# Issuing the output stores of a fused cross-covariance attention and mixture-of-adapters kernel from one queue, with the last outputs in seven pieces

## The chip, the cores and the metric

The kernel runs on one core of a Trainium2 chip. The metric is the device time of one execution in microseconds (us), lower is better. The kernel before takes 256.47 us, the median of three runs (256.42 to 256.54).

## What is computed

The inputs q, k and v are [4, 6400, 256] in float32. For each of the four batches, the columns of q and k are normalised over the 6400 tokens, a 256 x 256 matrix of their products goes through a softmax over its rows, and v is multiplied by it. The 25600 rows that come out then go through a mixture of eight adapters of rank 16, of which each row uses its best two:

```python
qn = q / (norm(q, axis=1) + 1e-6);  kn = k / (norm(k, axis=1) + 1e-6)
a  = softmax(kn.transpose(0, 2, 1) @ qn / tau)        # [4, 256, 256]
x  = (v @ a).reshape(25600, 256)
w  = softmax of the two largest of x @ w_gate          # 8 experts
out = x + sum over those two e of w_e * ((x @ A[e]) @ B[e])
```

The output is 25600 x 256 in float32, 26.2 MB.

## The kernel before

**Tiles.** A batch's 6400 tokens are 50 chunks of 128 (token = 50 x partition + chunk). Two chunks make a pair; there are 100 pairs, numbered u = 0 to 99, 25 to a batch. Pairs go in groups of five, for which gating is worked out at once; the last batch's are of 5, 5, 5, 5, 3 and 2 pairs. In this text G0 to G17 are the eighteen groups of pairs 0 to 89, five pairs each.

**Stages.** First the products and squares of batch 0 (`gram`, `norm`, `square`) run as its q and k arrive. Then a loop over slots takes one pair a slot: TensorE transposes its part of v (`transposes`, copied out of PSUM by VectorE or ScalarE), works out z (`z_gz`, L470), transposes the gated z back (`gz_t`, L494; copied by VectorE at L500, or from slot 100 on by ScalarE at L498), and adds both products into y (`y_mm` L486, `delta` L506). Beside that, up to slot 67, the loop carries the products of the following batch. The order of all instructions is written out by hand, and each engine runs its own in that order.

**Loads.** GpSimd issues all loads of q, k and v but the first; they convert float32 to bfloat16 on their way.

**Stores.** ScalarE copies each pair's y from PSUM into its group's tile `ys` (L510), 2 KB of each partition for a pair. A full group of five is 128 rows of 10,240 bytes, 1,280 KB. `delta` appends the full group to the list `unsent`, and `send`, called once a slot after `delta`, issues the oldest while more than `keep` are unsent. `keep` is 7 up to slot 67 and falls by one every four slots to 0 at slot 95. While `keep` is not 0 ScalarE issues the store, and SyncE when it is 0. By this ScalarE issues G0 to G14 and SyncE G15, G16 and G17. ScalarE issues in the order of its own program, between its copies; SyncE has nothing else to do, so its issues go out as soon as what they wait for is there. The last ten pairs, 90 to 99, are stored one at a time by SyncE at L513, 256 KB each, straight after their copies. They are called s0 to s9 here.

**Semaphores.** The 33 DMAs that SyncE and ScalarE issue (five first loads of SyncE, eighteen groups, ten single pairs) share eight completion semaphores in turn. A DMA that takes a semaphore waits until the DMA that had it before, eight places earlier, has landed: until all sixteen increments of that one have come, one from each of the sixteen DMA engines. s5 has the semaphore of G14 before it.

**Buffers.** `ys` has nine buffers. A group's first copy waits until the store of the group nine tiles earlier has landed.

Of the kernel before, what the change touches and what calls it, by code (L numbers as in the profile page):

```python
# [16 lines left out]
def kernel(  # L17
# [16 lines left out]
    nc = tc.nc  # L34
# [11 lines left out]
    NPAIR = NC // 2  # L46
    NPT = B * NPAIR
    GRP = 5
# [11 lines left out]
    out_v = out.rearrange("(b p c) d -> b p c d", b=B, p=P)  # L60
# [23 lines left out]
    for b, (first, last) in GRAM.items():  # L84
        n = last - first + 1
# [30 lines left out]
    def piece(kind, c):  # L116

        if kind == "qk":
            return divmod(c, PC)
        s = 0  # L120
        while c >= VP[s]:
            c -= VP[s]
            s += 1
        return s, c

    def used(kind, b, c, n):
        left[kind][where[kind, b, piece(kind, c)[0]]] -= n
# [220 lines left out]
    free_banks = [False]  # L348
    unsent = []

    def transposes(g, eng):

        b, p = divmod(g, NPAIR)
        gr = groups[g]
        if "vT" not in gr:
            gr["vT"] = vt_pool.tile([P, CC, 2 * GRP, P], BF16, tag="vT", name="vT")
        s, o = piece("v", 2 * p)
        vt = tiles["v"][b, s]
        full = ps_t.tile([P, 512], FP32, tag="pt", name="vT_ps")
        pt = full[:, 0:256].bitcast(BF16).rearrange("p (c t) -> p c t", c=CC)  # L360
        i = 0
        for sc in range(2):
            for ic in range(CC):
                nc.tensor.matmul(pt[:, ic, sc * P:(sc + 1) * P],  # L364
                                 vt[:, o + sc, ic * P:(ic + 1) * P], ident,
                                 is_transpose=True, start=(i == 0), stop=(i == 3))
                i += 1
        used("v", b, 2 * p, 2)
        w = 2 * (g - gr["f"])
        dst = gr["vT"][:, :, w:w + 2, :]  # L370
        src = pt.rearrange("p c (s t) -> p c s t", s=2)
        if eng == "act":
            nc.scalar.copy(dst, src)  # L373
        else:
            nc.vector.tensor_copy(dst, src)  # L375
        gr["full"] = full
        pr[g] = {"vT": dst, "w": w}
# [125 lines left out]
    def delta(u):  # L503
        r, gr = pr.pop(u), groups[u]
        for sc in range(2):
            nc.tensor.matmul(r["y"][:, sc, :], r["gzT"][:, sc, :], ball_sb, start=False,  # L506
                             stop=(sc == 1), skip_group_check=True)
        if "ys" not in gr:
            gr["ys"] = y_pool.tile([P, 2 * GRP, C], FP32, tag="ys", name="ys")
        nc.scalar.copy(gr["ys"][:, r["w"]:r["w"] + 2, :], r["y"])  # L510
        if u >= NPT - 2 * GRP:
            c0 = 2 * (u % NPAIR)
            nc.sync.dma_start(out_v[gr["b"], :, c0:c0 + 2, :], gr["ys"][:, r["w"]:r["w"] + 2, :])  # L513
        elif u == gr["f"] + gr["n"] - 1:
            unsent.append(gr)

    def send(keep):


        eng = nc.scalar if keep else nc.sync  # L520
        while len(unsent) > keep:
            gr = unsent.pop(0)
            c0, n = 2 * (gr["f"] - gr["b"] * NPAIR), 2 * gr["n"]
            eng.dma_start(out_v[gr["b"], :, c0:c0 + n, :], gr["ys"][:, 0:n, :])
# [43 lines left out]
    while nz < NPT or zq is not None or dq is not None:  # L568
# [12 lines left out]
        u = None  # L581
        if nz < min(slot, NPT) and groups[nz]["ready"]:
            u = nz
# [7 lines left out]
        if slot < NPT and not behind:  # L591
            transposes(slot, "dve" if items or f is chain3 else "act")
        if dq is not None:
            delta(dq)
        dq, zq = zq, u
        send(max(0, min(DEFER, DEFER - (slot - GRAM[B - 1][1]) // 4)))
        if behind:
            deal(0.3)
# [52 lines left out]
```

## Time and profile before

| | |
|---|---|
| median of three runs | 256.47 us (256.42 to 256.54) |
| the profiled execution's own time | 256.67 us |
| its span in the profile | 254.9 us |
| mean granted TensorE clock | 0.971 |
| busy: TensorE matmul, ScalarE, VectorE, GpSimd | 219.1, 176.3, 152.6, 32.5 us |
| bytes read from and written to HBM | 78.91 and 26.21 MB |
| store queue of ScalarE (q10): packets, MB | 2160, 19.66 |
| queue of SyncE (q1): packets, MB | 3488, 7.87 |
| ScalarE's last copy of y (L510) ends | 246.3 us |

The profile is of one execution. Times are from the start of its span. Sixteen DMA engines move all transfers; each queue has a ring on every one of them, and a store of 128 rows puts eight rows on each. A row is one packet; after its rows each engine writes one packet of 4 bytes, the increment of the semaphore. The share of DMA in a table is the mean busy share of the sixteen; it can pass 1 a little, since the packets of one engine overlap by 4 ns. "SPq" and "ACTq" stand for the issuing sequencers of SyncE and ScalarE, and "landing" is the time from issue to the last increment.

### The profile page before, as it was taken

Reading aid. Unit: us, or ns where it says so; the run is one execution under the profiler, and the core shown is the slowest. Engines: PE = TensorE matmul, PEld = TensorE weight load, DVE = VectorE, ACT = ScalarE, POOL = GpSimd, SP = SyncE. Lnnn points to the kernel's source line nnn. Section 1 sums busy time; section 2 is a strip of 40 time slices with the busy share of each in tenths; the row PEclk is TensorE's granted clock in tenths of the full one; section 3 lists DMA queues with packets and bytes.
Section 4 is the critical chain, followed back from the end, with each engine's and each line's share of the span. In section 5 each row is a group of like instructions: output and inputs, shape, how many; then the busy total and the mean of one; then the engine's idle time right before and its main releaser. Section 6 shows DMA issues by size and latency. Waiting matters only on the chain.

```text
span 254.9 us, 7402 instructions
## 1 busy us (share of the span) xinstructions
PE 219.1 (86%) x3106; PEld 189.2 (74%) x3106; DVE 152.6 (60%) x577; ACT 176.3 (69%) x290; POOL 32.5 (13%) x67
## 2 busy tenths in 40 slices
PE   0787792986999999999999999989999899999950
PEld 0444460875998878989999779879997799999930
DVE  1322335463757769676686685747587876778720
ACT  2434344676687797877976978778866777887850
POOL 8031221121112102020111011000000200000000
PEclk9999998697999999999999999999999999999996
DMA  7999999999999999999999999999999999999986
GB/s 210 225 215 216 212 217 214 213 215 216 213 213 215 221 209 214 221 209 218 211 219 213 214 297 233 259 270 284 252 299 295 382 331 356 425 425 418 425 359 231
DMA packets 14177, 66.80 MB, mean 262 GB/s; under 512 B 2624, under 2 KB 2752, under 8 KB 10816
## 3 DMA queue, kind: packets, MB, share of 16 engines
q0 software_dynamic: 8496, 38.80, 74.6%
q10 hardware_dynamic: 2160, 19.66, 18.7%
q1 hardware_dynamic: 3488, 7.87, 8.5%
q8 instruction: 24, 0.39, 0.6%
q14 instruction: 9, 0.07, 0.1%
HBM read 78.91 MB, written 26.21 MB: 412 GB/s over the span
## 4 chain that ended last, share of the span: by engine, by line
DMA 43%; PE 43%; DVE 5%; ACT 2%; POOL 2%; issue 2%; DVEq 0%; ACTq 0%; POOLq 0%
DMA vt<-in_v_dram 21%; PE y_ps L486 11%; DMA qk<-in_k_dram 9%; DMA qk<-in_q_dram 8%; PE acc L217 7%; PE y_ps L506 5%; DMA out_dram<-ys 5%; PE zg L470 5%; PE vT_ps L364 5%; PE zg L494 3%; PE vT_ps L385 3%; PE nrm L234 2%; DVE gz L474 1%; PE nrm L228 1%; POOL qk L148 1%
## 5 line engine op out<-in xcount | busy, mean ns | idle before, releaser
L207 ACT ACTIVATE sq<-qk 128x1024 bf16<-128x1024 bf16 x87 | 89.6, 1054 | 22.7 <-DMA qk<-in_k_dram 17.4
L217 PE MATMUL acc<-qk 128*128 128x256 bf16 x400 | 74.1, 286 | 15.3 <-DMA qk<-in_k_dram 8.8
L510 ACT COPY ys<-y_ps 128x512 f32<-128x512 f32 x100 | 58.7, 587 | 22.8 <-PE y_ps L506 19.3
L486 PE MATMUL y_ps<-a_bf,vT 128*128 128x256 bf16 x400 | 59.9, 272 | 0.3 <-ACT ys L510 0.3
L217 PEld LDWEIGHTS <-qk 128*128 128x128 bf16 x400 | 34.3, 101 | 25.2 <-DMA qk<-in_k_dram 11.4
L474 DVE TENSOR_TENSOR gz<-zg,gate 128x256 bf16<-128x256 f32 x100 | 41.7, 418 | 14.4 <-PE zg L470 12.9
L375 DVE COPY vT<-vT_ps 128x512 bf16<-128x512 bf16 x63 | 26.7, 424 | 29.0 <-PE vT_ps L364 28.3
L364 PE MATMUL vT_ps<-ident,vt 128*128 128x128 bf16 x400 | 39.5, 222 | 2.2 <-DMA vt<-in_v_dram 1.9
L234 PEld LDWEIGHTS <-sq 128*128 128x128 bf16 x600 | 36.1, 98 | 7.0 <-ACT sq L207 3.0
L470 PE MATMUL zg<-wa_sb,vT 128*128 128x128 bf16 x400 | 38.5, 219 | 1.2 <-DVE gzT L500 1.0
L506 PE MATMUL y_ps<-ball_sb,gzT 128*128 128x256 bf16 x200 | 38.2, 273 | 0.0
L234 PE MATMUL nrm<-ones_bf,sq 128*128 128x1 bf16 x600 | 35.7, 165 | 1.2 <-ACT sq L207 1.2
L486 PEld LDWEIGHTS <-vT 128*128 128x128 bf16 x400 | 33.5, 97 | 3.1 <-issue 0.4
L364 PEld LDWEIGHTS <-vt 128*128 128x128 bf16 x400 | 30.0, 99 | 5.2 <-DMA vt<-in_v_dram 2.7
L373 ACT COPY vT<-vT_ps 128x512 bf16<-128x512 bf16 x37 | 21.7, 587 | 10.2 <-PE vT_ps L364 8.9
L494 PE MATMUL zg<-ident,gz 128*128 128x128 bf16 x200 | 27.7, 221 | 1.1 <-DVE gz L474 0.6
L470 PEld LDWEIGHTS <-vT 128*128 128x128 bf16 x400 | 26.0, 97 | 3.3 <-issue 2.2
L500 DVE COPY gzT<-zg 128x256 bf16<-128x256 bf16 x90 | 25.3, 281 | 0.0
L148 POOL DMA_DIRECT2D qk<-in_q_dram x21 | 11.5, 547 | 88.4 <-ACT sq L207 19.4
L209 DVE TENSOR_TENSOR sq<-qk 128x1024 bf16<-128x1024 bf16 x13 | 9.1, 697 | 22.2 <-DMA qk<-in_k_dram 14.2
L151 POOL DMA_DIRECT2D vt<-in_v_dram x17 | 9.0, 534 | 65.7 <-PE y_ps L506 49.2
L494 PEld LDWEIGHTS <-gz 128*128 128x128 bf16 x200 | 15.2, 98 | 2.9 <-DVE gz L474 2.5
(61 smaller groups left out, 182.6 us busy)
## 6 DMA issues: line engine op xcount, KB each, us to landing
out_dram<-ys ACTq DMA_DIRECT2D x15, 1280.0 KB, 13.7
qk<-in_q_dram POOLq DMA_DIRECT2D x18, 640.0 KB, 21.2
qk<-in_k_dram POOLq DMA_DIRECT2D x18, 640.0 KB, 23.4
vt<-in_v_dram POOLq DMA_DIRECT2D x5, 1024.0 KB, 28.4
out_dram<-ys SPq DMA_DIRECT2D x3, 1280.0 KB, 10.8
vt<-in_v_dram POOLq DMA_DIRECT2D x3, 1152.0 KB, 26.2
vt<-in_v_dram POOLq DMA_DIRECT2D x6, 512.0 KB, 22.2
out_dram<-ys SPq DMA_DIRECT2D x10, 256.0 KB, 5.9
```

The costliest lines, as they stand in the source:

```text
L207: nc.scalar.activation(sq, src, ACT.Square)
L217: nc.tensor.matmul(acc[b][:, ic, :], t[:, 1, o, ic * P:(ic + 1) * P], t[:, 0, o, :], start=(c == 0 and ic == 0), stop=(c == NC - 1), skip_ ...
L234: nc.tensor.matmul(nrm[b][:, j:j + 1], sq[:, w, c % 2, ic * P:(ic + 1) * P], ones_bf[:, 0:1], start=(c == 0 and j == 0), stop=(c == NC - 1 ...
L364: nc.tensor.matmul(pt[:, ic, sc * P:(sc + 1) * P], vt[:, o + sc, ic * P:(ic + 1) * P], ident, is_transpose=True, start=(i == 0), stop=(i = ...
L375: nc.vector.tensor_copy(dst, src)
L470: nc.tensor.matmul(z[:, sc, :], r["vT"][:, ic, sc, :], st[b]["wa"][:, ic, E:E + ER], start=(sc == 0 and ic == 0), stop=(sc == 1 and ic == ...
L474: nc.vector.tensor_tensor(out=gz.rearrange("p c (e r) -> p c e r", e=E), in0=z.rearrange("p c (e r) -> p c e r", e=E), in1=gr["gate"][:, r ...
L486: nc.tensor.matmul(y[:, sc, :], r["vT"][:, ic, sc, :], st[b]["a"][:, ic, :], start=(sc == 0 and ic == 0), stop=False, skip_group_check=True)
L494: nc.tensor.matmul(gt[:, sc, :], r["gz"][:, sc, :], ident, is_transpose=True, start=(sc == 0), stop=(sc == 1))
L500: nc.vector.tensor_copy(gzT, gt)
L506: nc.tensor.matmul(r["y"][:, sc, :], r["gzT"][:, sc, :], ball_sb, start=False, stop=(sc == 1), skip_group_check=True)
L510: nc.scalar.copy(gr["ys"][:, r["w"]:r["w"] + 2, :], r["y"])
```

## The change

All whole groups, G15 to G17 too, are issued by ScalarE. Pairs 90 to 99 are still issued by SyncE, in seven pieces, called p0 to p6 here: pairs 90-91, 92-93, 94, 95-96, 97, 98, 99. Three of the seven are of two pairs (512 KB, rows of 4,096 bytes), four of one pair.

```diff
+    LAST = {NPT - 9: 4, NPT - 7: 4, NPT - 6: 2, NPT - 4: 4, NPT - 3: 2, NPT - 2: 2, NPT - 1: 2}
...
         nc.scalar.copy(gr["ys"][:, r["w"]:r["w"] + 2, :], r["y"])
-        if u >= NPT - 2 * GRP:
-            c0 = 2 * (u % NPAIR)
-            nc.sync.dma_start(out_v[gr["b"], :, c0:c0 + 2, :], gr["ys"][:, r["w"]:r["w"] + 2, :])
+        if u in LAST:
+            n = LAST[u]
+            c0, w = 2 * (u % NPAIR) + 2 - n, r["w"] + 2 - n
+            nc.sync.dma_start(out_v[gr["b"], :, c0:c0 + n, :], gr["ys"][:, w:w + n, :])
+        elif u >= NPT - 2 * GRP:
+            pass
         elif u == gr["f"] + gr["n"] - 1:
             unsent.append(gr)
...
-        eng = nc.scalar if keep else nc.sync
+        eng = nc.scalar
```

In the built programs the instructions of TensorE, VectorE and GpSimd, and their order, are the same. ScalarE has three DMA issues more: G15 and G16 one after the other, after the copy of pair 84 (slot 95), and G17 after the copy of pair 89 and ahead of the gzT copy that follows it. Each but G15 waits for the copy just ahead of it. SyncE has seven store issues where it had thirteen. G0 to G14 stand where they stood. There are 30 DMAs on the eight semaphores in place of 33: p4, p5 and p6 wait for G14, G15 and G16 to land.

## Prediction

> **What bounds the kernel now.** I read the page's slices of the span first, for the DMA row.
>
> ```profile
> DMA  7999999999999999999999999999999999999986
> GB/s 210 225 215 216 212 217 214 213 215 216 213 213 215 221 209 214 221 209 218 211 219 213 214 297 233 259 270 284 252 299 295 382 331 356 425 425 418 425 359 231
> ```
>
> The DMA engines are full from the second slice on. The change touches only the stores from G15 on, so I read the end: where the chain of waits ends, and then a table of stretches of that end.
>
> ```profile
> 245.75 0.58 ACT ys L510
> ```
>
> The chain of waits ends at 246.33 us with the last copy of y. The chain follows instructions; the transfer behind that copy is not in it, and 8.6 us of the span of 254.9 follow. That end is read from DMA alone:
>
> ```profile
> core 0: us, PE busy (x) PEld busy (x) DVE busy (x) ACT busy (x) POOL busy (x), PEclk, DMA share, GB/s
> 226.00:246.00 20.00, 19.27 (x259) 17.18 (x256) 13.08 (x58) 16.57 (x38) 0.00 (x0) 1.00 1.01 420
> 246.00:247.00 1.00, 0.00 (x0) 0.00 (x0) 0.00 (x0) 0.34 (x1) 0.00 (x0) 1.00 0.77 301
> 247.00:248.00 1.00, 0.00 (x0) 0.00 (x0) 0.00 (x0) 0.00 (x0) 0.00 (x0) 1.00 0.65 252
> 248.00:249.00 1.00, 0.00 (x0) 0.00 (x0) 0.00 (x0) 0.00 (x0) 0.00 (x0) 1.00 0.94 361
> 249.00:251.00 2.00, 0.00 (x0) 0.00 (x0) 0.00 (x0) 0.00 (x0) 0.00 (x0) 0.86 1.04 397
> 251.00:252.00 1.00, 0.00 (x0) 0.00 (x0) 0.00 (x0) 0.00 (x0) 0.00 (x0) 0.50 0.90 344
> ```
>
> Up to 246 us the sixteen engines are full of stores. Then there is a hole: for 3 us the shares are 0.77, 0.65 and 0.94, though the outputs of s5 to s9 are computed. The queue's own waits tell why:
>
> ```profile
> SPq L513 <- DMA out_dram<-ys: 5.4, 2, 3.5
> SPq L646 <- DMA out_dram<-ys: 3.6, 1, 3.6
> ```
>
> SyncE's single stores wait 5.4 us, in two waits, for older stores to land. The records of single issues show the longer one: s5 is issued at 247.41 us, when its semaphore's last owner, G14, has landed (247.35), while its data was there at 242.2. s6 to s9 follow at 247.84, 248.31, 248.82 and 249.31. This is what the change seems to mend.
>
> The question is whose hole it is, and the sixteen increments of each landing answer it. G9 lands between 218.94 and 222.34 us, s0 between 244.05 and 247.76, s4 between 246.63 and 250.33, and s9 between 252.01 and 253.56. So six engines are about 3.4 to 3.7 us ahead of the slowest from 219 us on, ahead of all that is changed. Those six ran dry and filled the hole with idling. The slowest engine never did: from s4 to s9 its landings stand at 250.33, 250.97, 251.64, 252.28, 252.93, 253.56, steps of 0.63 to 0.67 us, which is eight packets of 0.080 us and an increment. Counted from G9's landing on it, 222.34, it has 31.22 us to the end. Its work in that time is G10 to G17, 8 x (8 x 0.381 + 0.006) = 24.43 us, and s0 to s9, 10 x 0.646 = 6.46 us, together 30.89; the other 0.33 us is no idling but slower packets (one in sixteen or so takes 0.40 to 0.47 us, and an instruction packet of 16 KB takes 0.95). **So the bound of the end is the backlog of bytes on the slowest engine**, not the issues.
>
> **The change part by part.** I sum against the profiled execution, 256.67 us, which is 0.20 over the median of 256.47.
>
> *Three mergers.* Six of the single pairs become three stores of rows of 4,096 bytes. Before has no such store. On one engine 10,240 bytes take 0.381 us and 2,048 bytes 0.080 us (the records' 385 and 84 ns less 4 of overlap). The straight line between gives 0.1552 for 4,096, so a merger saves 16 x 0.080 - 8 x 0.1552 = 0.038 us and one increment of 0.007. Three save 0.13 us. The ends: at the rate of the 2 KB rows 0.02, at that of the 10 KB rows 0.20. I take 0.13, because SyncE's first loads, rows of 4,096 bytes too, have 0.159 us as their commonest packet, less 4 ns the line's value. These are on the slowest engine and on the path.
>
> *G15, G16 and G17 into ScalarE's queue.* The same packets go through the same engines, alone in a ring instead of alternating. From 219 to 226 us, with ScalarE's ring alone, the table of stretches has 430 GB/s; with both rings of 10 KB rows, 226 to 240, it has 422. So the order costs or gains at most 2%, and part of that is instruction packets (at 226.2, 230.5 and 232.0 us). I take nothing. The six engines ahead don't run dry either: at 229 us ScalarE's ring still holds part of G12 and all of G13 and G14, so G15, issued at about 229 where SyncE issued it at 222.52, comes in time.
>
> *The issues on ScalarE.* Each of the fifteen there takes 0.34 us (338 ns, 429 at most). The nearest rows for a bad case are SyncE's, up to 1.17 us. Behind them wait ScalarE's next copies:
>
> ```profile
> 228.75 0.59 ACT L510 COPY ys<-y_ps 128x512 f32<-128x512 f32 x1
> 229.98 0.58 ACT L373 COPY vT<-vT_ps 128x512 bf16<-128x512 bf16 x1 [0.64 <-PE vT_ps L364]
> ...
> 235.46 0.59 ACT L510 COPY ys<-y_ps 128x512 f32<-128x512 f32 x1
> 235.99 0.37 ACT L498 COPY gzT<-zg 128x256 bf16<-128x256 bf16 x1
> 236.65 0.58 ACT L510 COPY ys<-y_ps 128x512 f32<-128x512 f32 x1 [0.28 <-PE y_ps L506]
> ```
>
> G16 waits for the copy of pair 84 (229.34) and takes 0.34: 229.7, while ScalarE waited for TensorE until 229.98 anyway. G17 comes after the copy of pair 89 (236.05) and moves the gzT copy from 235.99 to about 236.4; 0.28 us of idling behind it takes part, and about 0.15 us may reach the last copy: 246.5 in place of 246.34. At 1.17 each it would be 2.5. Neither is on the path: the slowest engine must have p6's packets only when the rest is written, 253.1 - 0.65 = 252.45 us, and from issue to first packet s5 took about 0.9 us, so p6 may be issued as late as 251.5. Its last condition, the landing of G16, comes on the slowest engine at 222.34 + 7 x 3.05 + 1.25 (p0 beside it) + 0.33 = 245.3. The cover is 251.5 less 246.9, 4.6 us; without it the 0.15 to 2.5 us would count in full.
>
> Here the Trainium skill speaks against the change: "DMA: Bandwidth & Descriptors", section "Issuing engines are not separate DMA queues", says that DMAs of all issuers interleave on the same sixteen engines and that several issuers save just the sequencer's time. By this rule, without the cover, three issues given to ScalarE cost 3 x 0.34 = 1.0 us, and the time would be some 257.3. The trace agrees on the interleaving (422 against 430 GB/s) and hides the price.
>
> *Fewer, larger stores, and the wait that goes.* s5's wait of 5 us disappears, and what is late next is the slowest engine, which had work throughout: nothing gained. The same skill page, section "Anatomy of one DMA — SWDGE (gpsimd) path", gives about 2.0 us fixed for a DMA; three fewer, if they ran one after the other, would bring 6 us and 250.3. The rows say that it doesn't add up: back to back the single stores land 0.65 us apart.
>
> *SyncE's end.* It then waits for its DMAs (the second row of waits above) and for the barriers, from 253.57 to 254.9. Those eight waits stay.
>
> Sum: 256.67 - 0.13 = 256.54 for the profiled execution; against the median **256.34 us**.
>
> **The rivals.** *A, my forecast: the backlog of the slowest engine sets the end.* For it: unbroken landings at 0.65 us. Against it: nothing that I found.
>
> *B: the hole sets the end.* If all engines shared the idling, closing it is worth 3 x 1.01 - (0.77 + 0.65 + 0.94) = 0.67 us, with the mergers 0.80: 255.67. For it: the hole exists, and SyncE's issues do get earlier. Against it: the slowest engine has no hole. It would take a path by which the six idle engines held up the slow ones, and packets of 84 ns during and after the hole show none.
>
> *C, on the other side: ScalarE is held by its own queue.* Five stores outstanding on that queue are seen at 214.80 us (G7 to G11, issue 0.34 us). In the changed kernel G16 is the sixth if G11 still lands late. If the sequencer must wait for room, G16 waits for G11 (230.84 at worst, 1.4 us), G17 for G12 (236.87, 0.8 us), and with three issues of 1.17 less the idling of 0.92 the copies come 4.8 us later, just the cover of 4.6. Beyond that each microsecond counts; a stall of 6 us gives 257.7. Against it: SyncE's ring held seven stores of as many packets at 249.31 us (s3 to s9) with issues of 0.5 us.
>
> *That it doesn't do what it says:* SyncE's last pieces might still wait, now for G14 to G16. On the slowest engine that changes nothing, so the time is A's.
>
> **How the numbers follow.** A has 0.79, B 0.15, C 0.06. A's own range is the mergers' bounds and an instruction packet of 0.95 us falling on another engine or on the slowest, half of which I allow: 255.9 to 256.9. B lowers the low end to 255.5. C is left out. A measurement of this kernel can tell about 0.2%, 0.51 us, from no change: A lies within it, B below (faster 0.15), C above (slower 0.06).
>
> **What would show it.** Right: ScalarE's queue has 18 stores and SyncE's 7, packets fall by 3 x (128 + 16) = 432, SyncE's last issue comes before 248 us instead of 249.31, the six fast engines end near 249.7 instead of 252, DMA's share falls in steps from there, and the last landing stays within 0.3 us of 253.4. Wrong: the last landing comes more than 0.5 us earlier (B), or ScalarE's last copy later than 250 us (C). The forecast fails above all if the spread among the sixteen engines, 3.4 us at 222 us, isn't the same in the changed kernel.

## The result and the profile after

The changed kernel takes 256.03 us (255.87 to 256.22, 22 runs) against 256.44 of the kernel before (22 runs beside it): 0.41 us less, ratio 0.9983, 95% interval 0.9977 to 0.9988. The forecast was 256.34, in a range from 255.5 to 256.9, and a change within 0.2%. The change is 0.17% and the time lies in the range, but the gain is three times the 0.13 us that the forecast was built from. Two thirds of it came from a place that the forecast had put down as unchanged.

The profiled execution's span is 254.1 us (254.9 before). First the slices of the page:

```profile
DMA  7999999999999999999999999999999999999995
GB/s 213 223 217 215 212 216 214 213 216 216 210 214 215 223 207 215 218 212 214 215 220 211 214 270 259 236 296 281 255 291 292 389 326 362 414 420 426 423 412 220
DMA packets 13745, 66.80 MB, mean 263 GB/s; under 512 B 2576, under 2 KB 2704, under 8 KB 10384
```

The DMA engines are as full as before, and the packets fell by 432, as counted ahead. The table of stretches of the end (DMA's share and GB/s are the last two columns):

```profile
226.00:246.00 20.00, 19.03 (x255) 16.93 (x251) 12.91 (x57) 16.37 (x38) 0.00 (x0) 1.00 1.01 423
246.00:247.00 1.00, 0.00 (x0) 0.00 (x0) 0.00 (x0) 0.09 (x1) 0.00 (x0) 1.00 1.02 424
247.00:248.00 1.00, 0.00 (x0) 0.00 (x0) 0.00 (x0) 0.00 (x0) 0.00 (x0) 1.00 0.99 404
248.00:249.00 1.00, 0.00 (x0) 0.00 (x0) 0.00 (x0) 0.00 (x0) 0.00 (x0) 1.00 1.00 393
249.00:251.00 2.00, 0.00 (x0) 0.00 (x0) 0.00 (x0) 0.00 (x0) 0.00 (x0) 0.82 0.70 277
251.00:252.00 1.00, 0.00 (x0) 0.00 (x0) 0.00 (x0) 0.00 (x0) 0.00 (x0) 0.50 0.60 229
```

The hole from 246 to 249 us is gone (0.77, 0.65, 0.94 became 1.02, 0.99, 1.00), and it has moved: from 249 us on the share falls to 0.70 and 0.60, since the engines that are ahead now finish early. p6 lands on the first engine at 249.36 and on the last at 253.04 us. So closing the hole let the fast engines stop earlier. The last landing is 0.51 us earlier than in the trace of before (253.04 against 253.56), but that is one pair of executions: the four traces of kernels with ten single stores have it between 253.32 and 253.62, the six with the seven pieces between 253.04 and 253.42. SyncE's last issue is at 246.12 us (249.31 before).

Now the queue's own waits from 247 us on, which show what I had overlooked. Columns: who waited for what, us in total, times, longest.

```profile
SPq L651 <- DMA out_dram<-ys: 6.2, 6, 2.6
```

Before, the same row (L646) read 3.6 us in **one** wait; now it is 6.2 us in **six**. At its end SyncE waits for the eight semaphores one after the other, always in the same order. In before, the last DMA of all, s9, has the first semaphore in that order: the one wait ends at 253.57 us, and the seven waits behind it, all long fulfilled, still have to be gone through, at 253.64, 253.70, 253.76, 253.82, 253.88, 253.94 and 254.00: 7 steps in 0.43 us, 0.061 each. In after, the last piece has the sixth semaphore: six waits really wait, the last of them until 253.06, and just two steps follow (253.12, 253.18). From the last landing to the end of the span it is 1.33 us in before and 1.03 in after. Which semaphore the last DMA gets is decided by the number of DMAs: 33 before, 30 after, on eight semaphores in turn.

### The profile page after: what moved, and what is told of

Same layout as the page of the kernel before. It is cut to its first block, busy times and chain, and to the rows that moved or that the text cites. A ratio compares the mean times of both kernels' runs of the same rounds, so it can differ in the third digit from the quotient of the medians.

```text
span 254.1 us, 7393 instructions
## 1 busy us (share of the span) xinstructions
PE 220.4 (87%) x3106; PEld 190.2 (75%) x3106; DVE 152.7 (60%) x577; ACT 176.1 (69%) x290; POOL 33.0 (13%) x67
## 4 chain that ended last, share of the span: by engine, by line
PE 58%; DMA 25%; DVE 7%; ACT 3%; issue 2%; POOL 1%; DVEq 0%; POOLq 0%; ACTq 0%
DMA qk<-in_k_dram 20%; PE y_ps L488 15%; PE acc L217 11%; PE zg L472 7%; PE y_ps L508 7%; PE vT_ps L366 6%; DMA out_dram<-ys 5%; PE zg L496 4%; PE nrm L234 3%; PE vT_ps L387 3%; ACT sq L207 2%; DVE gz L476 2%; ACT ys L512 1%; DVE lm L422 1%; DVE e L418 1%
```

## The experiments

Each kernel's time stands against that of before on the same chip at the same time (256.52 us for the first four, 256.55 for the next four, 256.54 for the last three).

**Taking the change apart.** `e1_merge_only` leaves G15 to G17 to SyncE:

```diff
-        eng = nc.scalar
+        eng = nc.scalar if keep else nc.sync
```

> The seven pieces of SyncE as in the change, but G15 to G17 are left to SyncE as before: two rings of 10 KB rows again. Before is 256.44 us, after 256.03. Theory A (the slowest engine's packets alone set the end): the mergers bring 0.13, so 256.31, and the move to one ring must then bring its 0.28 by something on the slowest engine. Rival R (two rings cost something by themselves): 256.31 too, but slow packets or a lag that grows in the stretch from 226 to 240. Rival H (the hole of before set the end): the hole is partly there still, p5 waits for G14, so more than 256.2. If the whole gain comes from the pieces: 256.03.

Measured 256.15 us, 0.37 under before (ratio 0.9982, 0.9974 to 0.9991). The seven pieces alone bring what the whole change brings. p5 does wait for G14 here and is issued at 247.53 us, with DMA shares of 0.90 from 247 to 249 us; it costs nothing that these runs can tell.

`e2_move_only` is before with the one line `eng = nc.scalar`.

> G15 to G17 go to ScalarE's queue, but pairs 90 to 99 are stored singly, ten issues, as before. s7 must wait for G17 to land, so SyncE's last issues come late again, near 248 to 250 us, and the six engines ahead run dry. Theory A: that costs nothing; without the mergers the time is 0.13 over after, 256.16, if the move brings the other 0.28, and 256.44 if it doesn't. Rival H (the hole sets the end): 256.4 or more, with s9 landing about 0.4 us later than p6 did in after.

Measured 256.53, ratio 1.0003 (0.9994 to 1.0012): the move by itself brings nothing, and costs nothing. Its last single store is issued at 249.07 us. It has 33 DMAs and one last wait, as before:

```profile
SPq L646 <- DMA out_dram<-ys: 3.8, 1, 3.8
```

Rival H, too, allowed 256.4 or more, so this run does not separate the hole from theory A; the runs on the last waits below do.

So the whole gain is in the pieces, but more than the mergers' 0.13. Three explanations were left: the hole, chance in the one trace of before, or the last waits.

**Fewer pieces still.** `e3_three_pieces`:

```diff
-    LAST = {NPT - 9: 4, NPT - 7: 4, NPT - 6: 2, NPT - 4: 4, NPT - 3: 2, NPT - 2: 2, NPT - 1: 2}
+    LAST = {NPT - 6: 10, NPT - 3: 6, NPT - 1: 4}
```

> After, but pairs 90 to 99 go in three pieces, of 5, 3 and 2 pairs (rows of 10, 6 and 4 KB), issued later than the single ones were: at about 241, 244 and 246 us. Theory A: on the slowest engine the three take 3.05 + 1.85 + 1.25 = 6.15 us in place of 6.33, so 0.18 less than after, 255.85, and the later issues cost nothing since each comes before that engine has run out. Rival H (issue and landing of the last piece set the end): the last piece is twice as large, 0.6 us later or more: 256.6.

Measured 256.18, 0.34 under before (0.9986, 0.9977 to 0.9995), and not under after. This miss gave the clue. It should have won 0.31 us on before from the packets alone, and 0.28 more if what after had gained on top came with the pieces; it won only the first. Its 26 DMAs put the last piece on the second semaphore: two real waits, six steps behind the last landing, 1.27 us from there to the end:

```profile
SPq L651 <- DMA out_dram<-ys: 6.2, 2, 5.0
```

**Was it chance?** `e0_before_again` is before, for a second trace.

> The kernel before once more, for a second trace. Theory A: one engine's landings end 0.2 to 0.4 us behind the second slowest again, as s9's 253.56 stood against 253.22. If that was chance in one execution, the last landing stands within 0.1 us of the second.

It was chance: the last landing is at 253.42 us, the one before it, on another engine, at 253.38. The 0.34 us by which one engine was behind in the first trace changes from execution to execution (0.33 us in the trace of `e9_after_plus2`, under 0.1 in that of after). The time from the last landing to the end does not: 1.34 us, as in the first trace.

**ScalarE's cover.** `e4_all_act` has ScalarE issue the seven pieces too:

```diff
-            nc.sync.dma_start(out_v[gr["b"], :, c0:c0 + n, :], gr["ys"][:, w:w + n, :])
+            nc.scalar.dma_start(out_v[gr["b"], :, c0:c0 + n, :], gr["ys"][:, w:w + n, :])
```

> After, but ScalarE issues the seven pieces as well, each behind its own copies, so that its sequencer waits for each copy before it goes on. The last piece has the same semaphore as in after. Theory A (the slowest engine has work until 252.4 us): the copies come up to 2 us later and nothing is lost, 0.4 us under before, as after. Rival C (ScalarE's queue holds it up, and that reaches the end): more than 0.5 us over after.

Measured 256.17, 0.38 under before (0.9984, 0.9974 to 0.9993), as after. The timeline of ScalarE shows what it was charged:

```profile
247.24 0.34 ACTq L516 DMA_DIRECT2D out_dram<-ys  x1
247.62 0.58 ACT L512 COPY ys<-y_ps 128x512 f32<-128x512 f32 x1 [0.41 <-PE y_ps L508]
248.24 0.34 ACTq L516 DMA_DIRECT2D out_dram<-ys  x1
```

The last copy ends at 248.20 us, 2.1 later than in after, and the last piece is issued at 248.24. The last landing is at 253.18: the cover holds at least that far.

**The last waits by themselves.** `e5_before_plus7` and `e6_after_plus3` touch no store. They cut one 128 KB load at the start of the kernel into pieces of rows, which shifts the turn of the semaphores for all that follows (and adds seven or three small issues at the start). In before it becomes eight loads, in after four (the edit shown is that of `e5_before_plus7`):

```diff
-    nc.sync.dma_start(bst, moe_B.rearrange("e r d -> (e r) d"))
+    for lo, hi in [(0, 16), (16, 32), (32, 48), (48, 64), (64, 80), (80, 96), (96, 112), (112, 128)]:
+        nc.sync.dma_start(bst[lo:hi, :], moe_B.rearrange("e r d -> (e r) d")[lo:hi, :])
```

> Before, with nothing changed in any store; only the 128 KB load of moe_B at the start goes in eight DMAs in place of one, so that there are 40 DMAs on the eight semaphores and s9 has the last of them instead of the first. Theory E (SyncE's last waits go through the semaphores in a fixed order, 0.061 us each; in before the last landing has the first semaphore and seven waits come after it, in after the sixth and two come after it): 7 x 0.061 = 0.43 us under before. Rival P (the gain of the pieces is in the packets and engines alone): 0 to 0.1 us over before.

Measured 256.16, 0.39 under before (0.9987, 0.9979 to 0.9996): with before's own ten stores, nearly the whole gain of the change. The hole is still there, in the table of stretches:

```profile
247.00:248.00 1.00, 0.00 (x0) 0.00 (x0) 0.00 (x0) 0.00 (x0) 0.00 (x0) 1.00 0.66 252
```

So with a share of 0.66, as in before, the time is nearly that of after. From the last landing (253.62, no earlier than in before) to the end it is 0.90 us.

> After, with the load of moe_B in four DMAs, so that there are 33 DMAs as in before and p6 has the first semaphore. Theory E: five more waits after the last landing, 0.30 us over after, so about 0.1 us under before (the mergers' 0.13 alone). Rival P: as after, 0.4 us under before.

Measured 256.42, 0.13 under before (0.9994, 0.9986 to 1.0003), so about 0.3 us of after's gain were taken away again by cutting a load at the other end of the kernel. The hole of before is closed here, as in after:

```profile
246.00:247.00 1.00, 0.00 (x0) 0.00 (x0) 0.00 (x0) 0.00 (x0) 0.00 (x0) 1.00 1.00 416
247.00:248.00 1.00, 0.00 (x0) 0.00 (x0) 0.00 (x0) 0.00 (x0) 0.00 (x0) 1.00 1.00 408
248.00:249.00 1.00, 0.00 (x0) 0.00 (x0) 0.00 (x0) 0.00 (x0) 0.00 (x0) 0.60 0.98 389
```

This settles rival B. With the hole closed, the mergers made and the seven waits of before behind the last landing, the gain is 0.13 us, at most 0.36 by the interval, where B asked for 0.80. The two rows of waits from 249 us on, first of `e5_before_plus7`, then of `e6_after_plus3`:

```profile
SPq L647 <- DMA out_dram<-ys: 3.3, 6, 0.6
```

```profile
SPq L652 <- DMA out_dram<-ys: 7.0, 1, 7.0
```

In the first the waits end one by one with the landings, 0.6 us apart; in the second a single wait of 7.0 us comes first and seven steps follow.

**Putting it together.** `e7_three_plus6` is three pieces with the last one on the last semaphore (seven loads in place of one).

> Three pieces (5, 3 and 2 pairs), with the load of moe_B in seven DMAs, so that the last piece has the last semaphore. Theory E: six waits less after the last landing than with three pieces alone, 0.37 us less, so 0.7 us under before. Rival P: as three pieces alone, 0.34 us under before.

Measured 255.81, 0.74 under before (0.9974, 0.9964 to 0.9985). Against `e5_before_plus7`, which has its last DMA on the last semaphore as well and stood beside it, it is 0.35 us less: that is the larger mergers, of which 0.31 was expected, together with the move to one ring, which `e2_move_only` showed to be worth nothing, and the closed hole.

The last three stood side by side: after itself, after with its last piece moved to the last semaphore (three loads in place of one), and the kernel of `e7_three_plus6`.

> The changed kernel beside the next two on one chip. Theory E (mergers 0.13, five waits less after the last landing 0.30): 0.43 us under before, as it measured 0.41.

> After, with the load of moe_B in three DMAs, so that p6 has the last of the eight semaphores in place of the sixth. Theory E: two waits less after the last landing, 0.12 us under after, 0.55 under before. If the order of the last waits doesn't matter: as after.

> Three pieces with the last piece on the last semaphore. Theory E: 0.31 from the mergers and 0.43 from seven waits less, 0.74 under before, 0.31 under after; it measured 0.74 under before on another occasion.

Measured 256.13 (0.9984, 0.9975 to 0.9993), 256.00 (0.9979, 0.9970 to 0.9987) and 255.79 (0.9971, 0.9960 to 0.9982): 0.41, 0.54 and 0.75 us under before. The intervals of neighbours overlap, so no single step of 0.1 us is shown by itself. The table of all kernels is the evidence: two terms, packets on the slowest engine and 0.061 us for each wait behind the last landing, give every one of them to within 0.06 us. The fourth column, the time from the last landing to the end of the span, is read from the traces alone: 1.33 to 1.34 us with seven waits, 1.27 with six, 1.02 to 1.03 with two, 0.90 to 0.91 with none.

| kernel | DMAs | waits behind the last landing | from it to the end, us | packets, us | waits, us | sum | measured |
|---|---|---|---|---|---|---|---|
| before (e0 again, trace only) | 33 | 7 | 1.33, 1.34 | 0 | 0 | 0 | 0 |
| after (e8 again) | 30 | 2 | 1.03, 1.02 | -0.13 | -0.30 | -0.43 | -0.41, -0.41 |
| e1, pieces alone | 30 | 2 | 1.02 | -0.13 | -0.30 | -0.43 | -0.37 |
| e2, move alone | 33 | 7 | 1.34 | 0 | 0 | 0 | +0.01 |
| e3, three pieces | 26 | 6 | 1.27 | -0.31 | -0.06 | -0.37 | -0.34 |
| e4, all by ScalarE | 30 | 2 | 1.03 | -0.13 | -0.30 | -0.43 | -0.38 |
| e5, before, 7 loads more | 40 | 0 | 0.90 | 0 | -0.43 | -0.43 | -0.39 |
| e6, after, 3 loads more | 33 | 7 | 1.33 | -0.13 | 0 | -0.13 | -0.13 |
| e9, after, 2 loads more | 32 | 0 | 0.90 | -0.13 | -0.43 | -0.56 | -0.54 |
| e7, e10, three pieces, 6 loads more | 32 | 0 | 0.90, 0.91 | -0.31 | -0.43 | -0.74 | -0.74, -0.75 |

The last kernel is the best of all: 255.8 us.

## Why the prediction was right in its case and wrong in a term

The measured 256.03 us lies in the range, and inside A's own (255.9 to 256.9) by 0.13. That room had been given for an instruction packet and for the bounds of the mergers; that it also covered a term that nobody had named was luck. Two of the signs said ahead fell on the wrong side in the trace of after: the last landing is 0.36 us from 253.4, not within 0.3, and 0.51 us earlier than in before, just past the 0.5 that was to speak for B. One pair of traces is too few for such a sign, since last landings of like kernels differ by 0.3 to 0.4 us.

*The backlog of the slowest engine sets the end: right.* In after the landings of the last pieces on the slowest engine stand 0.64 us apart (251.13, 251.77, 252.41, 253.04), with no hole. Counted from G9's landing at 222.29 it has 30.75 us to the end; the work counted ahead was 30.76. The near match is luck: in the six traces with the seven pieces this time is 30.75 to 31.05 us, in the four with ten stores 30.88 to 31.34. The spread among the engines at G9, on which all this hung, is 222.29 less 218.59, 3.7 us (3.4 in before, 3.0 to 4.0 over all the traces). The records do not name the engine of an increment; that the last ones belong to one engine is read from their even steps.

*Three mergers, 0.13 us: right as far as it can be seen.* In after the stores' rows of 4,096 bytes took 0.159 us (the median of 384), as read ahead from SyncE's loads. `e6_after_plus3` has the mergers with as many waits behind the last landing as before and measures 0.13, with an interval that includes no change; the larger mergers of three pieces measure 0.35 against 0.31. No run closes the hole without a merger, so what little the hole might be worth is contained in these figures.

*G15 to G17 in one ring, nothing: right* (`e2_move_only`, ratio 1.0003). With ScalarE's ring alone the stretch from 226 to 240 us has 427 GB/s where two rings had 422, without any gain in time. What the Trainium skill says in "DMA: Bandwidth & Descriptors", section "Issuing engines are not separate DMA queues", that DMAs of all issuers run on the same sixteen engines and interleave, agrees with it.

*The issues on ScalarE, hidden: right.* In after the two issues that wait for a copy read so:

```profile
228.51 0.59 ACT L512 COPY ys<-y_ps 128x512 f32<-128x512 f32 x1
229.13 0.62 ACTq L529 DMA_DIRECT2D out_dram<-ys  x1
229.79 0.58 ACT L375 COPY vT<-vT_ps 128x512 bf16<-128x512 bf16 x1 [0.69 <-PE vT_ps L366]
...
235.21 0.59 ACT L512 COPY ys<-y_ps 128x512 f32<-128x512 f32 x1
235.83 0.34 ACTq L529 DMA_DIRECT2D out_dram<-ys  x1
236.27 0.37 ACT L500 COPY gzT<-zg 128x256 bf16<-128x256 bf16 x1 [0.47 <-DVE dm L431]
236.53 0.59 ACT L512 COPY ys<-y_ps 128x512 f32<-128x512 f32 x1
```

G16's issue took 0.62 us, not 0.34, and the copy of vT behind it starts 1.28 us after the copy of y in place of 1.23. At G17 the next copy of y starts 1.32 us after the one before it in place of 1.19, 0.13 us against the 0.15 forecast. ScalarE's last copy ends at 246.09 us, no later than in before (246.34). The cover of 4.6 us was counted from a last landing at 253.1, where the same text has 253.4 elsewhere; with 253.4 it would be 4.9, and nothing hangs on the difference.

*SyncE's end, "Those eight waits stay": wrong, and this is the step that failed.* The waits stay eight, but not all of them are paid for. Only those that come behind the last landing are, and three DMAs fewer moved the last landing's semaphore from the first place to the sixth: five steps of 0.061 us, 0.30 us. The term was zero in the sum. It could have been read from before: its row of waits at the end says *one* wait of 3.6 us, and eight semaphores were to be waited for.

*Rival B, the hole:* refuted by `e6_after_plus3`, which closes the hole and gains 0.13 us, and by `e5_before_plus7`, which keeps it and gains 0.39. *Rival C, ScalarE held by its queue:* its condition, a sixth store outstanding, did not come up in after, where at most five are. In `e4_all_act` there are six from 245.34 us on, the issues then take 0.34 us each, and nothing was lost; a longer queue was not tried. The longest issue of ScalarE was 0.62 us in after and 0.77 in any run (`e2_move_only`). *The Trainium skill's about 2.0 us fixed for a DMA* (the same page, section "Anatomy of one DMA — SWDGE (gpsimd) path"), which that section gives for DMAs that GpSimd issues, is no guide to stores of SyncE that queue behind each other: by it three fewer would bring 6 us, and beside equal waits at the end they brought 0.13 (`e6_after_plus3`).

What stays open is why six of the sixteen engines are ahead. Landings in before spread by 1.4 us for the store that ends at 155.7 us, by 4.8 at 194.7 and 5.5 at 211.0, while the loads still run (their last packet is at 218.9), so the lead grows beside the loads. Which transfers make it was not tried.

## What to carry to other kernels

When transfers queue to the end, ask of a hole in the DMA's share which engine has it: the sixteen increments of one store after another tell whether the last engine ever idled, and if it didn't, an earlier issue is not to be expected to help. Then read the end of the program as well: here the final waits are gone through in a fixed order, so let the DMA that lands last have the semaphore that is waited for last; here it was enough to cut an unrelated load into pieces. And don't put a term to zero because its instructions stay: what counts is how many of them lie behind the event that they wait for.

## What the runs showed of the hardware

A wait on a semaphore that has long been reached still takes SyncE 0.061 us, and at the end of the program nothing hides it. The packets of stores cost 0.080, 0.155, 0.230 and 0.381 us for 2, 4, 6 and 10 KB on one engine (medians of 84, 159, 234 and 385 ns less 4 of overlap; the 6 KB rows are those of `e3_three_pieces`), a straight line with 5 ns at its foot. With ScalarE's ring full of 10 KB rows, a store issued on SyncE's empty ring sees its first packet late: 3.6 us after issue for G15 in before (222.52, 226.15), 3.4 for p0 in after, 1.8 for the first of the three pieces in `e3_three_pieces`. s5 in before, which came when some engines were idle, needed about 0.9.
